# Down products in threes and twos, and a larger carry-over in the column stage: a fused spectral filter and gated MLP

## The chip, the cores and the metric

The kernel runs on one core of a Trainium2 chip. The metric is the device time of one execution in microseconds (us); times given as a median come from three runs. One further execution was taken by the profiler: its time is 1315.97 us, and the span that the trace covers is 1314.2 us. All stamps of the trace are microseconds from the start of that span.

## What is computed

The reference mixes two branches, cut here to what matters (S = 2048 tokens, D = 576, hidden width 4608, all float32):

```python
X = rfft2(A_x, axes=(-2, -1))                 # 2048 x 576
a = irfft2(X * (w_r + 1j * w_i), (S, D))      # spectral branch
h = gelu(B_x @ w_gate) * (B_x @ w_up)         # 2048 x 4608
b = h @ w_down
g = sigmoid((A_x * gate_w).sum(-1, keepdims=True))
y = g * a + (1 - g) * b
```

## The kernel before, in words

**Matmul branch.** TensorE does the products of B in float32 by splitting operands into a high and a low part. Hidden columns come in pairs of 128-wide blocks, tokens in two halves of 1024. The first two pairs of the first half are done plainly (`normal`). The other 34 (16 pairs of the first half, 18 of the second) are the *groups* of `products(b, k)` (L1397): the gate and up products of a pair with two times 512 tokens are made from **seven products** in the manner of Strassen, named in the loop at L1440 `a11, a12, s2, s3, s1, a22, s4`. The text calls them the first to the seventh. Each has two halves (s = 0, 1), each half is 7 matmuls of 128x512 into one PSUM bank (`seven`, six at L1390 and one at L1392). Partial results are copied from PSUM by ScalarE (`copy`, whose records carry L237): after the first product both halves are copied from one pair of banks into the other (`px<-pgu` or `pgu<-px`), after the third and the fourth into `xraw`. The second product goes on adding to the banks that the first one's copies read, and the fourth to the banks that the third one's copies read, so the second product's half s waits for the first product's copy of half s, and the fourth's for the third's.

**Down products.** A finished group gives eight *downs* (`down`, L992), 12 matmuls of 128x288 each (L975) into one of two PSUM buffers `pdn`. ScalarE evicts a down with the factor 1 - g (`stg<-pdn`, L1008) into one of four `stg` buffers, and GpSimd's queue issues the transfer that adds it to the sum `yd` in DRAM (`put`, L990). The eight downs of a group are carried in the list `pend` and done in the next group, so many after each product as `downs` (L1439) says. The opening group and the last one have rows of their own.

**Weights.** `prep` makes the weight tile of a product three products ahead: VectorE forms sums (L1362), ScalarE the high part (`gub<-low` or `slot<-low`, L237), VectorE the low part (L1377), and SP's queue fetches tails (L1369).

**Spectral branch.** It is written as Python generators that hand out a few VectorE and ScalarE instructions at a time: rows of the transform, then a *column stage* (`columns`, L291) whose 128-point transforms are 32 small TensorE products (L352, also into `pdn`), then the inverse rows for tokens 0 to 1023 (h = 0) and 1024 to 2047 (h = 1). At the end of each, `adds` (L700) scales eight blocks by g and adds them to `yd` through GpSimd's queue (L715); with h = 0 every second block is scaled by ScalarE (L712) and the others by VectorE (L714), out of five places that are used in turn.

**What sets the order.** Nothing reorders at run time: each engine runs its instructions in the order in which this program writes them. Between pieces of TensorE work (half a product, or a down) stands a *gap* (`gap`, `dealt`, L785). There the credit, which grows by 1.08 times the TensorE time passed and falls by what VectorE work costs, is cut to `cap` (2.0 us), and while it is positive the spectral generators give out instructions; `yield None` ends a generator's turn in that gap. In the column stage (`ops["ahead"]`) a second generator (`beside`) is served first, and a down's eviction is put off to the end of its gap. In that stage `HOLD` = 3 empty turns stand before the fourth step's next operand.

**The end.** In the last group the rest of the spectral work is handed out after the sixth product (`while gens`); then SP's queue loads blocks 12 to 15 of `yd` (`load_last(1)`, L1034), and the last eight downs (`finale`) are added to them on VectorE (L1045) and stored.

Of the kernel before, what the change touches and what calls it, by code (L numbers as in the profile page):

```python
# [28 lines left out]
UNIT = ROWS // 4  # L29
RATE = 1.08  # L30
STEP = 8
HOLD = 3
FIRST = 2
APART = (13, 14, 16, 17)
PAIRS = ((2, 3, 4, 5), (6, 7, 8, 9), (10, 11, 12, 13), (14, 15, 16, 17), (0, 1))
# [126 lines left out]
def _build(nc, tc, a):  # L162
    with ExitStack() as ctx:
# [127 lines left out]
        def columns():  # L291
# [90 lines left out]
            def beside():  # L382
                while not ops.get("turn"):
                    yield None
                yield from forward(1)
                for d in range(2):
                    yield from backward(d)
                    yield from forward(d + 2)
                for d in range(2, 4):
                    yield from backward(d)  # L390
# [11 lines left out]
            end = gub[BLOCK[1]][:, 2304:2560]  # L402
# [15 lines left out]
            yield from step()  # L418
            side.append(beside())
            ops["ahead"] = True  # L420
            for kb in range(16):
                was, more = kb > 0, kb + 1 < 16
                v = product(0, kb, xh, xl)
                if was:
                    copy(yh, vs)
                yield from step()
                copy(zr, v[:, 1, :NK])
                copy(t0, v[:, 0, :NK])
                yield from step()
                if was:  # L430
                    vec.tensor_tensor(yl, vs, f(yh), ALU.subtract)
                vec.tensor_tensor(zi, t0, zr, ALU.subtract)
                vec.tensor_tensor(zr, t0, zr, ALU.add)
                yield from step(1.67 if was else 0.91)
                turned(vs, z, 1.0)
                u = product(1, kb - 1, yh, yl) if was else None
                yield from step()
                if was:
                    copy(two(tile_of(kb - 1)), u[:, :, :NK])
                    done[0] = kb - 1  # L440
                vec.tensor_tensor(z, z, w0, ALU.mult)
                vec.tensor_tensor(vs, vs, w1, ALU.mult)
                yield from step(1.52)
                if more:
                    if kb == 3:
                        yield from waits(HOLD)
                    while made[0] < (kb + 1) // 4:
                        yield None
                    copy(xh, tile_of(kb + 1))
                vec.tensor_tensor(z, z, vs, ALU.add)  # L450
                vec.tensor_tensor(vs2[:, 0], zr, zi, ALU.add)
                vec.tensor_tensor(vs2[:, 1], zr, zi, ALU.subtract)
                at(1, lambda kb=kb: load_ww(kb + 1, 0))
                at(2, lambda kb=kb: load_ww(kb + 1, 1))
                yield from step(1.67)
                if more:
                    vec.tensor_tensor(xl, tile_of(kb + 1), f(xh), ALU.subtract)
                yield from step(0.76)
                yield from waits(STEP - 7)
# [11 lines left out]
            done[0] = 15  # L471
            yield None
            ops["ahead"] = False
            for c in side.pop():
                yield c
            for e in range(2):
# [118 lines left out]
        def waits(n):  # L595
            for _ in range(n):
                yield None
# [167 lines left out]
        cap = [2.0]  # L765
# [296 lines left out]
        ops = {}  # L1062
# [336 lines left out]
        def products(b, k):  # L1399

            p, i = b.groups[k]
            j = p * NT + 2 * i
            u, u3 = ([xraw[:, 2 * q + s] for s in range(2)] for q in range(2))
            made = {}
            opening, end, turn = k == 0, k == len(b.groups) - 1, (p, i) == (0, NBLK - 1)
            if opening:
                at(6, lambda: credit.__setitem__(0, credit[0] - 2.0))
                for q in range(2 * len(PAIRS) - 2):
                    t = (free_low[:, 0:7 * P] if q % 2 == 0 else wtb[:, 0:7 * P]).rearrange("p (m k) -> p m k", m=7)
                    for n, fn in zip((-4, 6, 8, 9, 10), tail_piece(q + 2, t)):  # L1410
                        at(max(1, n + 12 * q), fn)

            def finish(name, x, o):
                g, v = x
                hold = made[name] = []

                def mult():
                    vec.tensor_tensor(o, o, v, ALU.mult)
                    credit[0] -= 0.69

                def gelu():
                    act.activation(o, g, AF.Gelu_apprx_tanh)

                wants = dict(c21=extra[1:], c22=extra[:1]).get(name, base)
                if end and name in ("c21", "c12"):
                    gelu()
                    seq((name, k), (1, mult), *split_h(o, hold, wants, True))
                else:
                    soon = 0 if end else 1
                    high, low = (fn for _, fn in split_h(o, hold, wants))  # L1430
                    late = name in ("c22", "c12") and not end
                    seq((name, k), (1 + late, gelu), (2 + (soon if name != "c21" else 0) + late, mult), (4 + soon + late - end, high), (5 + 2 * soon + late, low))

            def add(o, v):
                vec.tensor_tensor(o, o, v, ALU.add)
                credit[0] -= 0.69

            fore, acc = ([f() for f in fs] for fs in ((ps_gu, ps_gu), (lambda: ps_x(0), lambda: ps_x(1)))[::1 - 2 * (k % 2)])
            downs = (0, 0, 0, 0, 0, 1, 1) if opening else (2, 2, 2, 2, 2, 0, 0) if end else (1, 1, 1, 1, 1, 1, 2)  # L1439
            for n, (name, nd) in enumerate(zip(("a11", "a12", "s2", "s3", "s1", "a22", "s4"), downs)):  # L1440
                m = n + 3
                b.prep(k + m // 7, m % 7)
                if n == 0 and k:
                    b.load_d(k)
                if n == 4:
                    w, x = dns[:, j % 4:j % 4 + 2], b.both
                    copy(w[:, :, 0], x)

                    def rest_of(w=w, x=x):
                        vec.tensor_tensor(w[:, :, 1], x, f(w[:, :, 0]), ALU.subtract)  # L1450
                        credit[0] -= 1.35

                    seq(("dn", j), (5, rest_of))
                if n == 3 and opening:
                    b.more()
                if n == 0:
                    b.load(k + 1, "r11", "r21")
                elif n == 3:
                    b.load(k + 1, "r22")
                elif n == 4:  # L1460
                    b.load(k + 1, "r12")
                if n == 4:
                    fore = [ps_x(s) for s in range(2)] if k % 2 else [ps_gu() for _ in range(2)]
                ps = acc if n in (2, 3, 5) else fore
                for s in range(2):
                    soon = opening and n in (0, 2)
                    b.seven(ps[s], k, n, name, s, n in (0, 4), (lambda n=n, s=s: copy((acc, None, u)[n][s], ps[s])) if soon else None)
                    if n in (0, 2, 3) and not soon:
                        copy((acc, None, u, u3)[n][s], ps[s])
                    elif n in (4, 6):  # L1470
                        at(0 if end else 1, lambda x=(u3, u)[n // 2 - 2][s], y=ps[s]: add(x, y))
                if turn:
                    ops["turn"] = True
                    if n == 6:
                        for q, e in enumerate(ye):
                            at(60 + 6 * q, lambda e=e: pl.dma_start(yd[e[1]], ye[e], accum_op=ALU.add, max_dma_last_dim=D))
                    assert ops["kept"]
                    at(2, lambda name=name: swap(name))
                if n in (1, 4, 5, 6):
                    finish(*{1: ("c11", fore, gl[0]), 4: ("c22", u3, u3[0]), 5: ("c21", acc, gl[1]), 6: ("c12", u, u[0])}[n])  # L1480
                for _ in range(nd):
                    if pend:
                        down(*pend.pop(0))
                if end and n == 5:
                    while gens:
                        credit[0] = 1.0
                        gap()
                    load_last(1)
            due(("dn", j))
            for tb, names in ((1, ("c21", "c22")), (0, ("c11", "c12"))):  # L1490
                d = (p, i, tb, tuple((j + q, made[names[q]], (names[q], k)) for q in range(2)))
                pend.extend((d, t) for t in range(4))
# [207 lines left out]
```

## Time and profile before

| | before |
|---|---|
| median of 3 runs (lowest to highest) | 1316.6 us (1315.26 to 1317.08) |
| the profiled execution: time, span | 1315.97 us, 1314.2 us |
| granted TensorE clock over the span | 0.997 |
| TensorE busy | 1300.6 us, 99% of the span, 7210 matmuls |
| VectorE, ScalarE, GpSimd busy | 1136.1, 832.7, 308.1 us |
| HBM read, written | 157.87, 137.88 MB |

A row of the timeline reads: start, duration, engine, line, operation, what is written from what, shapes, how many instructions are merged in it, and in brackets how long the engine had been idle before and what ended that. PE is TensorE, DVE VectorE, ACT ScalarE, POOL GpSimd, SP SyncE. Matmuls overlap, so the time between two starts, not the duration, says what one costs.

### The profile page before, as it was taken

What the parts mean: (1) busy time and instruction counts of PE and PEld (TensorE: products, weight loads), DVE (VectorE), ACT (ScalarE), POOL (GpSimd) and SP (SyncE); (2) the same over time, 40 slices, a digit from 0 to 9 for tenths busy, and PEclk for the clock granted to TensorE, in tenths of its full rate; (3) what the DMA queues carried; (4) which work ended last, traced back from release to release, by engine and by line L of the source; (5) the groups of instructions that cost most, each with busy time, mean ns of one, the idle gap of its engine ahead of it and who ended that gap; (6) DMA issues with size and microseconds to landing.
All of it is one profiled execution on the core that took longest, in us unless ns stands there. A gap on an engine that the chain in (4) does not pass through costs nothing.

```text
span 1314.2 us, 20538 instructions
## 1 busy us (share of the span) xinstructions
PE 1300.6 (99%) x7210; PEld 1152.4 (88%) x7210; DVE 1136.1 (86%) x1734; ACT 832.7 (63%) x1405; POOL 308.1 (23%) x392
## 2 busy tenths in 40 slices
PE   9999999999999999999999999999999999999996
PEld 7888888888888888888888888888888888888895
DVE  7899999988999988778878968767999997999974
ACT  5565665657565667768677876867656557556551
POOL 0011121212121111124310333333333314121131
PEclk9999999999999999999999999999999999999998
DMA  9779999896777799969985999999999979877789
GB/s 351 239 210 235 259 262 241 180 291 132 140 143 148 141 328 364 298 181 279 364 264 176 211 271 213 217 223 223 199 171 174 177 163 216 191 142 142 141 172 232
DMA packets 202392, 285.94 MB, mean 218 GB/s; under 512 B 18160, under 2 KB 118640, under 8 KB 201392
## 3 DMA queue, kind: packets, MB, share of 16 engines
q0 software_dynamic: 64848, 110.13, 48.7%
q1 hardware_dynamic: 137008, 174.06, 41.1%
q8 instruction: 56, 0.92, 0.3%
q10 hardware_dynamic: 432, 0.44, 0.1%
q14 instruction: 48, 0.39, 0.1%
HBM read 157.87 MB, written 137.88 MB: 225 GB/s over the span
## 4 chain that ended last, share of the span: by engine, by line
PE 91%; issue 4%; DMA 2%; POOL 1%; ACT 1%; DVE 0%; DVEq 0%; POOLq 0%; ACTq 0%; SPq 0%
PE pdn L975 32%; PE px L1390 23%; PE pgu L1390 23%; PE px L1392 4%; PE pgu L1392 4%; PE pdn L352 2%; POOL yd L990 1%; DMA yd<-wtb 1%; PE px L911 1%; DMA yd<-low 1%; PE pgu L911 0%; DMA low<-yd 0%; PE pgu L891 0%; PE pgu L892 0%; PE px L891 0%
## 5 line engine op out<-in xcount | busy, mean ns | idle before, releaser
L1008 ACT ACTIVATE stg<-pdn,omg 128x576 f32<-128x576 f32 x276 | 204.8, 743 | 327.5 <-PE pdn L975 206.5
L990 POOL DMA_DIRECT2D yd<-stg x232 | 201.6, 870 | 817.4 <-ACT stg L1008 787.3
L975 PE MATMUL pdn<-dn,hb 128*128 128x288 f32 x1356 | 199.5, 294 | 0.3 <-ACT rows L237 0.2
L975 PEld LDWEIGHTS pdn<-dn,hb 128*128 128x128 f32 x1356 | 191.7, 188 | 8.6 <-ACT rows L237 0.5
L1390 PE MATMUL pgu<-xhi,gub 128*128 128x512 f32 x480 | 149.2, 392 | 0.0
L975 PEld LDWEIGHTS pdn<-dn,ext 128*128 128x128 f32 x816 | 122.9, 189 | 17.1 <-DVE low L1045 7.4
L975 PE MATMUL pdn<-dn,ext 128*128 128x288 f32 x816 | 130.2, 295 | 7.0 <-DVE low L1045 7.0
L1390 PE MATMUL pgu<-til,gub 128*128 128x512 f32 x516 | 131.9, 391 | 0.0
L975 PE MATMUL pdn<-dn,gub 128*128 128x288 f32 x816 | 130.0, 295 | 0.0
L237 ACT ACTIVATE gub<-low 128x512 fp32r<-128x512 f32 (+1 forms) x163 | 101.0, 621 | 28.7 <-DVE low L1362 23.1
L975 PEld LDWEIGHTS pdn<-dn,gub 128*128 128x128 f32 x816 | 116.1, 189 | 0.0
L1377 DVE TENSOR_TENSOR gub<-low,gub 128x512 fp32r<-128x512 f32 x151 | 103.5, 685 | 8.5 <-ACT gub L237 6.9
L1390 PEld LDWEIGHTS pgu<-til,gub 128*128 128x128 f32 x516 | 94.5, 188 | 17.8
L1390 PE MATMUL px<-xhi,gub 128*128 128x512 f32 x344 | 106.9, 392 | 0.6 <-ACT xraw L237 0.6
L1390 PE MATMUL px<-til,gub 128*128 128x512 f32 x396 | 101.3, 391 | 0.0
L1390 PEld LDWEIGHTS pgu<-xhi,gub 128*128 128x128 f32 x480 | 86.4, 188 | 14.7 <-ACT px L237 0.3
L1390 PE MATMUL pgu<-xlo,gub 128*128 128x512 f32 x240 | 93.6, 390 | 0.0
L1390 PEld LDWEIGHTS px<-til,gub 128*128 128x128 f32 x396 | 72.3, 188 | 13.5
L1390 PEld LDWEIGHTS px<-xhi,gub 128*128 128x128 f32 x344 | 62.0, 188 | 11.9 <-ACT xraw L237 1.0
L975 PE MATMUL pdn<-dn,hx 128*128 128x288 f32 x444 | 70.2, 294 | 0.0
L1362 DVE TENSOR_TENSOR low<-low 128x512 f32<-128x512 f32 x98 | 67.4, 687 | 1.1 <-DMA low<-ws 0.3
L1390 PE MATMUL px<-xlo,gub 128*128 128x512 f32 x172 | 67.1, 390 | 0.0
(309 smaller groups left out, 2765.5 us busy)
## 6 DMA issues: line engine op xcount, KB each, us to landing
yd<-stg POOLq DMA_DIRECT2D x232, 288.0 KB, 5.3
low<-ws SPq DMA_DIRECT2D x114, 256.0 KB, 5.4
gub<-tails SPq DMA_DIRECT2D x179, 128.0 KB, 5.1
gub<-wd SPq DMA_DIRECT2D x68, 288.0 KB, 5.6
tails<-wtb SPq DMA_DIRECT2D x28, 448.0 KB, 5.6
ye<-stg POOLq DMA_DIRECT2D x32, 288.0 KB, 5.8
yd<-ye POOLq DMA_DIRECT2D x32, 288.0 KB, 8.0
slot<-tails SPq DMA_DIRECT2D x59, 128.0 KB, 4.9
```

The source lines that it names most:

```text
L237: act.activation(o, i, AF.Copy)
L352: pe.matmul(v[:, al, :NK], cc[d][2 * al + q], two(x)[:, al], start=n == 0, stop=n == 2)
L911: pe.matmul(ps[j][s], w[:, l, k, cs[s]], x0k, start=k == 0 and l == 0 and x is xhi, stop=k == 3 and x is xlo)
L975: pe.matmul(ps[half], h[:, l, c], d[:, q, half * HD:(half + 1) * HD], start=part == 0 and n == 0, stop=part == 1 and n == 2)
L990: pl.dma_start(yd[u], o, accum_op=ALU.add)
L1008: out = lambda: put(u, lambda o: act.activation(o.rearrange("p (c k) -> p c k", c=2), v[:, :, 0:HD], AF.Copy, scale=omg[:, u:u + 1]), i == ...
L1362: vec.tensor_tensor(o, p, q, ALU.subtract)
L1377: vec.tensor_tensor(v[:, 0:5:4], x, f(v[:, 1:4:2]), ALU.subtract)
L1390: pe.matmul(ps, l, x[:, t], start=first and t == 0 and q == 0, stop=False, skip_group_check=True)
L1392: pe.matmul(ps, w[:, 512 + P * s:512 + P * (s + 1)], xt, start=False, stop=True, skip_group_check=True)
```

## The change

Three edits. In groups that are neither the opening nor the last one, `downs` is replaced: outside the column stage three downs follow the second product, three the fifth and two the seventh; in the column stage it stays at one after each and two after the seventh. `popped` counts what was done, so that a group in which the stage begins or ends still does eight. The credit's cap is 3.0 in the column stage and 2.0 again after it. `HOLD` and its three empty turns are gone. Since lines went and came, L-numbers of the changed program differ by -1 to +3.

```diff
-HOLD = 3
...
             ops["ahead"] = True
+            cap[0] = 3.0
             for kb in range(16):
...
-                    if kb == 3:
-                        yield from waits(HOLD)
                     while made[0] < (kb + 1) // 4:
...
             ops["ahead"] = False
+            cap[0] = 2.0
...
+            popped = 0
             for n, (name, nd) in enumerate(zip(("a11", "a12", "s2", "s3", "s1", "a22", "s4"), downs)):
...
+                if not (opening or end):
+                    nd = (n + 1 + n // 6 if ops.get("ahead") else (0, 3, 3, 3, 6, 6, 8)[n]) - popped
+                    popped += max(0, nd)
                 for _ in range(nd):
                     if pend:
                         down(*pend.pop(0))
```

**First place: GpSimd's queue at the end of the program.** Before, the last twelve transfers into `yd`; L715 are the spectral branch's adds, L990 the downs' (`yd_151` to `yd_158` are the blocks 8 to 15):

```order
L990 DMA yd_151<-stg_84 128x576
L715 DMA yd_153<-wtb 128x576
L990 DMA yd_152<-stg_85 128x576
L715 DMA yd_154<-wtb 128x576
L715 DMA yd_155<-wtb 128x576
L990 DMA yd_153<-stg_86 128x576
L990 DMA yd_154<-stg_87 128x576
L715 DMA yd_156<-low 128x576
L715 DMA yd_157<-low 128x576
L715 DMA yd_158<-tmp 128x576
L715 DMA yd_151<-tmp 128x576
L715 DMA yd_152<-tmp 128x576
```

The last twelve of the changed program (L714 are the adds, L989 the downs'):

```order
L714 DMA yd_158<-tmp 128x576
L714 DMA yd_151<-tmp 128x576
L989 DMA yd_153<-stg_86 128x576
L989 DMA yd_154<-stg_87 128x576
L989 DMA yd_155<-stg_84 128x576
L989 DMA yd_156<-stg_85 128x576
L989 DMA yd_157<-stg_86 128x576
L989 DMA yd_158<-stg_87 128x576
L989 DMA yd_151<-stg_84 128x576
L989 DMA yd_152<-stg_85 128x576
L989 DMA yd_153<-stg_86 128x576
L989 DMA yd_154<-stg_87 128x576
```

Before, the adds are the very last; now ten downs, more than a group's worth, follow the last add.

**Second place: TensorE in the group that the adds of h = 0 fall into.** Before, from the down behind the second product to the fourth product (`px0`, `px1` are the banks of halves 0 and 1):

```order
L975 MATMUL pdn_10202<-dn_75,hb0_78 128x288 x6
L975 MATMUL pdn_10202<-dn_75,hb1_80 128x288 x6
L1390 MATMUL px0_10135<-til1_335,gub2_73 128x512 x6
L1392 MATMUL px0_10135<-til1_335,gub2_73 128x512
L1390 MATMUL px1_10136<-til1_335,gub2_73 128x512 x6
L1392 MATMUL px1_10136<-til1_335,gub2_73 128x512
L975 MATMUL pdn_10246<-dn_75,ext_911 128x288 x6
L975 MATMUL pdn_10246<-dn_75,gub2_73 128x288 x6
L1390 MATMUL px0_10135<-til1_335,slot_74 128x512 x6
L1392 MATMUL px0_10135<-til0_334,slot_74 128x512
L1390 MATMUL px1_10136<-til1_335,slot_74 128x512 x6
L1392 MATMUL px1_10136<-til0_334,slot_74 128x512
```

The changed program, in the group that its adds fall into, from the second of the three downs behind the second product to the fourth product (`pgu_9855` and `pgu_9856` are here the two banks):

```order
L974 MATMUL pdn_9926<-dn_75,hb2_79 128x288 x6
L974 MATMUL pdn_9926<-dn_75,hx_159 128x288 x6
L974 MATMUL pdn_9945<-dn_75,ext_911 128x288 x6
L974 MATMUL pdn_9945<-dn_75,gub2_73 128x288 x6
L1389 MATMUL pgu_9855<-til1_335,slot_74 128x512 x6
L1391 MATMUL pgu_9855<-til1_335,slot_74 128x512
L1389 MATMUL pgu_9856<-til1_335,slot_74 128x512 x6
L1391 MATMUL pgu_9856<-til1_335,slot_74 128x512
L1389 MATMUL pgu_9855<-til1_335,gub1_72 128x512 x6
L1391 MATMUL pgu_9855<-til0_334,gub1_72 128x512
L1389 MATMUL pgu_9856<-til1_335,gub1_72 128x512 x6
L1391 MATMUL pgu_9856<-til0_334,gub1_72 128x512
```

The down that stood between the third and the fourth product is gone from there; both write the same two banks.

**Third place: ScalarE in the same two groups.** Before (L712 scale blocks for the adds, L1008 evict downs, `xraw<-px` are the copies of the third and then of the fourth product):

```order
L712 ACTIVATE wtb<-rows,gs 128x576
L237 ACTIVATE xraw<-px_10135 128x512
L237 ACTIVATE gub_72<-low 128x2x256
L712 ACTIVATE low<-rows,gs 128x576
L237 ACTIVATE xraw<-px_10136 128x512
L1008 ACTIVATE stg_84<-pdn,omg 128x576
L712 ACTIVATE wtb<-rows,gs 128x576
L237 ACTIVATE hb_78<-gl_81 128x512
L237 ACTIVATE xraw<-px_10135 128x512
L237 ACTIVATE gub_73<-low 128x2x256
L712 ACTIVATE wtb<-rows,gs 128x576
L237 ACTIVATE xraw<-px_10136 128x512
```

The changed program (L711, L1007 and L236 are the same lines; L1421 is the GELU):

```order
L1007 ACTIVATE stg_86<-pdn,omg 128x576
L1421 ACTIVATE gl_81<-px_9853 128x512
L711 ACTIVATE low<-rows,gs 128x576
L1007 ACTIVATE stg_87<-pdn,omg 128x576
L711 ACTIVATE wtb<-rows,gs 128x576
L1007 ACTIVATE stg_84<-pdn,omg 128x576
L711 ACTIVATE wtb<-rows,gs 128x576
L236 ACTIVATE xraw<-pgu 128x512
L236 ACTIVATE hb_79<-gl_81 128x512
L236 ACTIVATE gub_73<-low 128x2x256
L236 ACTIVATE xraw<-pgu 128x512 x2
L236 ACTIVATE slot<-low 128x2x256
```

Before, the fourth and last L712 stood ahead of the fourth product's second copy; now it stands ahead of the third product's first copy.

## The prediction

> **What bounds the kernel now.** I read the page first, then the chain of waits, then the timeline wherever TensorE stood still. On the page:
>
> ```profile
> PE 1300.6 (99%) x7210; PEld 1152.4 (88%) x7210; DVE 1136.1 (86%) x1734; ACT 832.7 (63%) x1405; POOL 308.1 (23%) x392
> ```
>
> TensorE sets the time nearly everywhere, so an edit is worth what it changes in TensorE's standing still, or in the cost of a matmul. No matmul is added or removed. The place where TensorE stands still longest is shown by the end of the chain of waits:
>
> ```profile
> 1285.89 7.29 DMA yd<-low
> 1293.24 5.95 DMA low<-yd
> ```
>
> The last adds of the spectral branch are in flight to 1293.2; only then can SP load those sums for the last downs. In TensorE's timeline (start first, in brackets the idle time):
>
> ```profile
> 1288.01 0.95 PE L975 MATMUL pdn<-dn,ext 128*128 128x288 f32 x6
> 1288.80 0.95 PE L975 MATMUL pdn<-dn,gub 128*128 128x288 f32 x6
> ...
> 1290.39 0.95 PE L975 MATMUL pdn<-dn,gub 128*128 128x288 f32 x6
> 1291.68 1.06 PE L975 MATMUL pdn<-dn,ext 128*128 128x288 f32 x6 [0.34 <-DVE low L1045]
> 1292.58 0.95 PE L975 MATMUL pdn<-dn,gub 128*128 128x288 f32 x6
> 1300.17 1.81 PE L975 MATMUL pdn<-dn,ext 128*128 128x288 f32 x6 [6.64 <-DVE low L1045]
> 1301.78 1.64 PE L975 MATMUL pdn<-dn,gub 128*128 128x288 f32 x6
> 1303.22 1.07 PE L975 MATMUL px<-dn,hb 128*128 128x288 f32 x6
> ```
>
> Six matmuls take 0.79 from start to start (1288.01 to 1288.80). The five steps from 1290.39 to 1303.22 take 12.83 instead of 5 x 0.79 = 3.95, so this stall costs **8.9 us**. After the idle 6.64, two sixes took 1.61 and 1.44: 1.47 of the 8.9 is slow matmuls behind a long pause.
>
> **The change part by part, against the profiled 1315.97.**
>
> *The spectral branch ends earlier.* `HOLD`'s three empty turns and the lower cap go; in GpSimd's queue ten downs follow the last add, more than a group. So the load of blocks 12 to 15 no longer waits for an add. What is late next there is the last down's transfer to block 15, which was issued here:
>
> ```profile
> 1270.18 0.86 POOL L990 DMA_DIRECT2D yd<-stg  x1 [0.42 <-ACT stg L1008]
> ...
> yd<-stg POOLq DMA_DIRECT2D x232, 288.0 KB, 5.3
> ```
>
> It lands at about 1275.5, and with 5.95 for the load that is 1281.4, 8 us ahead of the first down of the finale that needs it (ends 1289.6). That covers it: **-8.9**.
>
> *The column stage itself* must pack the same work into less TensorE time:
>
> ```profile
> 560.00:875.00 315.00, 314.75 (x1786) 280.88 (x1785) 251.35 (x400) 238.78 (x401) 95.84 (x138) 1.00 0.94 242
> ```
>
> VectorE is busy 251 of 315 there (80%). Roughly 35 us, one group, goes; with that group's own VectorE work gone too it becomes about 84%, still under full, and TensorE idled only 0.25 in this stretch. I take 0, bounded by -0.25 and the price in the fourth rival.
>
> *Fewer changes between shapes.* A group, by the chain of waits:
>
> ```profile
> 1103.51 1.38 PE pgu L1390 x6
> ...
> 1105.12 1.36 PE pgu L1390 x6
> 1106.71 3.16 PE pdn L975 x24
> ...
> 1141.72 3.16 PE pdn L975 x24
> ```
>
> The half product behind a down takes 1.61 to the next half, the second half 1.59 (1105.12 to 1106.71). A change from downs to products so costs 0.02; seven a group become three. Of 32 groups that are neither first nor last, eight lie in the column stage (280 us of 35.0 each, 1106.71 to 1141.72): 24 x 4 x 0.022 = **-2.1** (0 if the 0.02 belongs to something else).
>
> *Copies that lose their cover.* This is the part that I hold against the change. Before, 1.58 of down lay between the first and the second product and between the third and the fourth, so a copy of half s had two pieces, 3.17, to finish in; now it has one half product, 1.59. Undisturbed it needs about 0.85 (0.25 from the end of TensorE's piece to ScalarE's start, as at 1273.67 to 1273.92 below, and 0.6 for itself) and costs nothing. But ScalarE runs in order, and the weight piece just ahead of it waits for VectorE:
>
> ```profile
> ACT gub L237 <- DVE low L1362: 23.1, 21, 2.8
> ...
> 314.06 0.95 PE L975 MATMUL pdn<-dn,hb 128*128 128x288 f32 x6
> 315.63 0.63 PE L1390 MATMUL px<-xhi,gub 128*128 128x512 f32 x2
> 315.71 0.63 ACT L237 ACTIVATE gub<-low 128x512 fp32r<-128x512 f32 x1 [2.40 <-DVE low L1362]
> 316.25 0.58 ACT L237 ACTIVATE pgu<-px 128x512 f32<-128x512 f32 x1
> ...
> 936.98 1.74 PE L975 MATMUL pdn<-dn,hb 128*128 128x288 f32 x12
> ...
> 938.24 0.58 ACT L237 ACTIVATE px<-pgu 128x512 f32<-128x512 f32 x1
> ```
>
> At 314 the second half of the first product ended at 314.06; the copy ended at 316.83. Under the new order the second product's second half is due at 314.06 + 1.59 = 315.65: a stall of 1.18 that the down hid. In the same way for all pairs outside the column stage I find eight places, at 314, 324, 359, 454, 489, 524, 902 and 937, with 1.18, 0.69, 0.41, 0.86, 1.56, 1.38, 1.69 and 0.25: **+8.0**. The VectorE work ahead of them is the same in both orders, moved by a gap or two, so I keep the sum; bounds are 0 (the lag falls elsewhere) and 11.
>
> *Third down of three.* It needs the first one's buffer:
>
> ```profile
> 1272.09 3.32 PE L975 MATMUL pdn<-dn,hb 128*128 128x288 f32 x24
> 1273.92 0.74 ACT L1008 ACTIVATE stg<-pdn,omg 128x576 f32<-128x576 f32 x1 [1.03 <-PE pdn L975]
> ```
>
> The first of these two ended at 1273.67, its eviction at 1274.66, and a third would start at 1275.25: 0.59 to spare. ScalarE must be late by more; bounded by 0 and 6 (a quarter of 48 places by 0.5), I take **+0.5**, near the quiet row.
>
> *The adds of h = 0* fall into another part of a group. Before:
>
> ```profile
> yd<-wtb POOLq DMA_DIRECT2D x9, 288.0 KB, 7.5
> ...
> 1084.27 0.59 ACT L1422 ACTIVATE gl<-pgu 128x512 f32<-128x512 f32 x1
> ...
> 1087.05 1.47 ACT L712 ACTIVATE low<-rows,gs 128x576 f32<-128x576 f32 x1
> 1088.90 0.74 ACT L1008 ACTIVATE stg<-pdn,omg 128x576 f32<-128x576 f32 x1
> 1090.00 0.85 POOL L990 DMA_DIRECT2D yd<-stg  x1 [2.63 <-ACT stg L1008]
> 1090.54 1.19 POOL L715 DMA_DIRECT2D yd<-wtb  x1
> 1098.03 1.47 ACT L712 ACTIVATE wtb<-rows,gs 128x576 f32<-128x576 f32 x1 [3.07 <-DMA yd<-wtb]
> 1099.08 0.39 PE L1392 MATMUL px<-til,gub 128*128 128x512 f32 x1
> 1099.36 0.63 ACT L237 ACTIVATE xraw<-px 128x512 f32<-128x512 f32 x1
> 1100.04 0.73 PE L1390 MATMUL px<-xhi,gub 128*128 128x512 f32 x2 [0.57 <-ACT xraw L237]
> ```
>
> The fourth L712 reuses the third add's place and waits until that transfer, issued at 1090.54, has landed. The copy behind it belonged to the fourth product and was needed by the sixth: TensorE lost 0.73 (0.96 from 1099.08 to 1100.04, where a matmul takes 0.23). Now the copy behind it is the third product's, which the fourth waits for. Counted from the end of the first of the three downs: 0.25 to its eviction, 0.74 for it, 0.59 GELU, 1.47 for the second L712, 0.74 for the next eviction, 0.36 and 0.54 in GpSimd's queue (as 1089.64 to 1090.00 and to 1090.54), 7.47 in flight, 1.47 for the fourth L712, 0.6 copy: 14.2. The fourth product is due after two downs and two halves, 3.16 + 3.18 = 6.3. That is 7.9, and 1.5 of slow matmuls as behind the 6.64 pause: **+9.4**, and **-0.7** for the old stall. VectorE waits there for another place too, but stands free before the copy is done. Behind the stalled fourth product all of TensorE's queue waits; the other engines catch up.
>
> Sum: 1315.97 - 8.9 - 2.1 + 8.0 + 0.5 + 9.4 - 0.7 = 1322.2. The median of the runs lies 0.6 above the profiled execution, so **1322.8**.
>
> **The rivals.** (1) *ScalarE's queue is short at the joints.* In threes, evictions no longer stand between a product and its copies. If that lets VectorE and ScalarE come to the joints with less than 1.59 of lag, the 8.0 is gone, and one eviction, 0.7, goes from the chain at the adds: 1322.8 - 8.7 = 1314.1, against 1316.6 faster by 0.2%. It decides from the point where the lag at those eight places falls under 1.59. Against it: at 314 ScalarE waited 2.40 for VectorE and not for an eviction. (2) *The adds' transfers land sooner.* The nearest quick row for this size is a plain store:
>
> ```profile
> yd<-stg SPq DMA_DIRECT2D x16, 288.0 KB, 2.2
> ```
>
> With 2.2 for 7.47 the stall is 2.6 without slow matmuls: 1322.8 - 9.4 + 2.6 = 1316.0. Against it stands the median of 7.5 of these very transfers. The Trainium skill, "DMA: Bandwidth & Descriptors", section "Anatomy of one DMA — SWDGE (gpsimd) path", fits 2.0 us plus bytes over 436e3 to a transfer issued by GpSimd, by my estimate 2.7 us for 288 KB; the sum by it would be 1316.5. The trace here has 7.5, nearly three times that. (3) *Both together*: 1307.3. (4) *The stage becomes VectorE's.* Were each of its 32 small products 0.2 late, 6.4 more: 1329.2. Against it the 84%. That the branch would not end earlier is excluded by the order of GpSimd's queue.
>
> The Trainium skill also says in "TensorE: Matmul & The Clock Gate", section "The HAM clock gate (the "warmup" mystery)", that the array's clock is halved after an idle window of about 3.4 us and returns after as long a busy one. The 1.47 behind the 6.64 is of that kind; by the page the pause at the adds would cost 1.7 behind it, 1323.0 in all, and several pauses of one or two us nothing.
>
> **How the numbers follow.** Forecast 0.57, rival 1 0.20, rival 2 0.10, rival 3 0.05, rival 4 0.08. About 0.2%, 2.6 us, can be told from no change: faster is under 1314.0, slower over 1319.2. Rival 1 at 1314.1 is half faster, half same; rival 3 is faster, and a fifth of rival 2: 0.10 + 0.05 + 0.02 = 0.17. Same: 0.10 + 0.08 and 0.05 of the forecast, if the copies cost 4 instead of 8: 0.23. Slower 0.60. The forecast's own range is 1318 to 1327 (copies 4 to 11, flight 5.3 to 8.0 as the rows for transfers into `yd` have it). To hold 8 in 10, the range takes in rivals 1 and 2 to 1312 and part of rival 4 to 1328:
>
> ```profile
> yd<-ye POOLq DMA_DIRECT2D x32, 288.0 KB, 8.0
> ```
>
> **What would show it.** Right: the finale's downs 0.79 a six without the 6.64; the half behind a down still 1.61; waits of the second and fourth product for ScalarE's copies, in sum near 8, and one of about 8 us behind the fourth scaling of h = 0. Wrong: no single TensorE wait over 3 us near 1050, TensorE's waits for copies under 3 in all, or a long wait still ahead of the finale.

## The result, and the profile after

The changed kernel takes **1333.2 us** (median of four runs, 1332.26 to 1334.14); the kernel before takes 1316.35 beside it (four runs, 1315.26 to 1317.08). The ratio is 1.0128, 95% interval 1.0115 to 1.0141: slower by about 17 us. The prediction had the sign and the two largest terms, the end and the adds; its 1322.8 was short by 10 us, and the result lies outside its range, which ended at 1328. The profiled execution of the changed kernel took 1332.48 us with a span of 1330.7, at a granted clock of 0.996.

The page's first line, busy time and instructions of each engine:

```profile
PE 1305.1 (98%) x7210; PEld 1153.0 (87%) x7210; DVE 1137.7 (85%) x1734; ACT 831.4 (62%) x1405; POOL 308.4 (23%) x392
```

All engines run as many instructions as before, and VectorE, ScalarE and GpSimd are busy as long as before, within 2 us. TensorE is busy 4.5 us longer, in matmuls that run slowly behind pauses; the rest of the 17 us are the pauses between its matmuls. What TensorE waited for (engine, line, what released it, then us in all, times, longest), of before the largest, and of after:

```profile
PE pdn L975 <- DVE low L1045: 7.0, 2, 6.6
```

```profile
PE pgu L1389 <- ACT xraw L236: 8.9, 2, 7.9
PE px L1389 <- ACT pgu L236: 5.2, 6, 1.6
PE pgu L1389 <- ACT px L236: 2.1, 2, 1.6
...
PE pdn L351 <- DVE tmp L431: 1.3, 1, 1.3
PE pdn L974 <- ACT stg L1007: 1.2, 2, 0.8
```

One wait of the end is gone, and waits for ScalarE's copies (L236) stand all over the program. To put each microsecond in its place I took from both traces, for every matmul, the time from its start to the next one's start, less what it is in undisturbed work (0.227 us for 512 columns, 0.132 for 288, 0.1345 for the stage's 290), and summed the excess by place (the program's first 10 us, 2.6 in both, are left out):

| place | before | after | difference | predicted |
|---|---|---|---|---|
| groups before the column stage | 0.1 | 3.9 | +3.8 | +6.1 (six of the eight copies) |
| column stage | 0.8 | 5.1 | +4.4 | 0 |
| behind the stage, up to the adds of h = 0 | 0.3 | 7.7 | +7.4 | +1.9 (two of the eight copies) |
| adds of h = 0 | 0.8 | 10.3 | +9.5 | +8.7 |
| last two groups and finale | 9.0 | 0.6 | -8.4 | -8.9 |
| single steps of 0.04 or less, all places | 4.1 | 4.3 | +0.2 | -2.1 |

The differences sum to 16.9 and the two profiled executions lie 16.5 apart, so the table holds all of it to 0.4. The prediction's column sums to 5.7; with its +0.5 for the third downs that is its 6.2.

**The end.** The finale in TensorE's timeline (start, duration, engine, line):

```profile
1313.79 0.95 PE L974 MATMUL pdn<-dn,ext 128*128 128x288 f32 x6
...
1319.36 0.95 PE L974 MATMUL pdn<-dn,gub 128*128 128x288 f32 x6
1320.15 0.97 PE L974 MATMUL px<-dn,hb 128*128 128x288 f32 x6
```

Eight steps in 6.36, 0.795 each: the 6.64 that stood here is gone, as foretold.

**The adds of h = 0**, timelines of ScalarE, GpSimd and TensorE together:

```profile
1062.73 0.74 ACT L1007 ACTIVATE stg<-pdn,omg 128x576 f32<-128x576 f32 x1 [1.80 <-issue]
1063.85 1.42 ACT L711 ACTIVATE low<-rows,gs 128x576 f32<-128x576 f32 x1
1065.18 0.73 ACT L1007 ACTIVATE stg<-pdn,omg 128x576 f32<-128x576 f32 x1
...
1067.78 0.85 POOL L989 DMA_DIRECT2D yd<-stg  x1 [1.98 <-issue]
1068.32 1.18 POOL L714 DMA_DIRECT2D yd<-wtb  x1
1068.65 0.39 PE L1391 MATMUL pgu<-til,slot 128*128 128x512 f32 x1
1075.02 1.34 ACT L711 ACTIVATE wtb<-rows,gs 128x576 f32<-128x576 f32 x1 [4.11 <-DMA yd<-wtb]
1076.27 0.58 ACT L236 ACTIVATE xraw<-pgu 128x512 f32<-128x512 f32 x1
1076.90 2.93 PE L1389 MATMUL pgu<-til,gub 128*128 128x512 f32 x6 [7.87 <-ACT xraw L236]
...
1080.06 2.26 PE L1389 MATMUL pgu<-til,gub 128*128 128x512 f32 x6
```

These are the links of the prediction in its order; their lengths differ, as the account of the prediction below says. The add issued at 1068.32 has landed by 1075.02, the fourth scaling reuses its place, the copy of the third product stands behind it, and the fourth product waits 7.87. Seven matmuls then take 3.16 (1076.90 to 1080.06) instead of 1.59.

**Copies that lost their cover.** The place at 314 of the kernel before, now:

```profile
315.39 0.68 DVE L1361 TENSOR_TENSOR low<-low 128x512 f32<-128x512 f32 x1
...
315.93 0.39 PE L1391 MATMUL px<-til,gub 128*128 128x512 f32 x1
316.11 0.63 ACT L236 ACTIVATE gub<-low 128x512 fp32r<-128x512 f32 x1 [2.28 <-DVE low L1361]
316.64 0.58 ACT L236 ACTIVATE pgu<-px 128x512 f32<-128x512 f32 x1
317.28 0.74 PE L1389 MATMUL px<-xhi,gub 128*128 128x512 f32 x2 [0.95 <-ACT pgu L236]
```

From 315.93 to 317.28 are 1.35 where 0.23 is usual: 1.12 lost, and 1.18 was foretold. Behind the stage there is more of it than foretold:

```profile
913.44 0.39 PE L1391 MATMUL px<-til,gub 128*128 128x512 f32 x1
913.66 0.64 ACT L236 ACTIVATE ext<-gl 128x512 fp32r<-128x512 f32 x1
914.20 0.70 ACT L236 ACTIVATE rows<-wtb 128x289 f32<-128x289 f32 x1
914.70 0.69 ACT L236 ACTIVATE pgu<-px 128x512 f32<-128x512 f32 x1
915.44 0.73 PE L1389 MATMUL px<-xhi,gub 128*128 128x512 f32 x2 [1.61 <-ACT pgu L236]
```

Here it is the inverse rows' own copy (`rows<-wtb`) and an operand's that stand ahead of the product's copy.

**The column stage.** VectorE's timeline, TensorE's at the same time, and the busy time in the stage (in this order PE, PEld, DVE, ACT, POOL):

```profile
618.20 1.56 DVE L266 TENSOR_TENSOR rows<-low,rows 128x580 f32<-128x580 f32 x2 [0.93 <-ACT low L251]
619.67 1.55 DVE L266 TENSOR_TENSOR rows<-rows,low 128x580 f32<-128x580 f32 x2
621.14 0.68 DVE L959 TENSOR_TENSOR hb<-gl,hb 128x512 fp32r<-128x512 f32 x1
621.75 0.76 DVE L431 TENSOR_TENSOR tmp<-wtb,tmp 128x580 fp32r<-128x580 f32 x1
622.56 0.40 PE L351 MATMUL pdn<-tmp 128*128 128x290 f32 x1 [1.26 <-DVE tmp L431]
```

```profile
565.00:846.00 281.00, 277.49 (x1578) 247.18 (x1577) 232.00 (x372) 216.70 (x367) 83.59 (x125) 1.00 0.92 248
```

VectorE is busy 232 of 281 there, 83%, which the prediction had as 84% and took for harmless. The small product starts at 620.86, and the operand that its third matmul needs (L431) stands in VectorE's queue behind four sums of the second generator (L266) and a product's own work. VectorE itself had stood idle for 0.93 ahead of these sums, for a step of ScalarE (L251), and the first half of that step (L250) had waited 0.90 for VectorE's sums before it (L259): the two hand work to each other.

**Longer runs of one shape.** Three downs in a quiet group:

```profile
1141.29 0.95 PE L974 MATMUL pdn<-dn,hb 128*128 128x288 f32 x6
...
1144.45 0.98 PE L974 MATMUL pdn<-dn,ext 128*128 128x288 f32 x6
...
1146.06 1.54 PE L1389 MATMUL pgu<-til,gub 128*128 128x512 f32 x6
```

The first two downs take 3.16 (1141.29 to 1144.45), the third 1.61 instead of 1.58.

### The profile page after: what moved, and what is told of

Its sections match the earlier page's. It is cut to its first block, busy times and chain, and to the rows that moved or that the text cites. A ratio compares the mean times of both kernels' runs of the same rounds, so it can differ in the third digit from the quotient of the medians.

```text
span 1330.7 us, 20521 instructions
## 1 busy us (share of the span) xinstructions
PE 1305.1 (98%) x7210; PEld 1153.0 (87%) x7210; DVE 1137.7 (85%) x1734; ACT 831.4 (62%) x1405; POOL 308.4 (23%) x392
## 4 chain that ended last, share of the span: by engine, by line
PE 71%; issue 13%; DVE 4%; DMA 4%; POOL 4%; ACT 4%; SPq 0%; POOLq 0%; DVEq 0%; ACTq 0%
PE pdn L974 25%; PE pgu L1389 17%; PE px L1389 17%; PE pgu L1391 3%; POOL yd L989 3%; PE px L1391 3%; DMA yd<-stg 2%; PE pdn L351 1%; POOL yd L714 1%; DMA gub<-wd 1%; ACT stg L1007 1%; DMA rows<-away 1%; DVE rows L266 1%; DMA home<-rows 1%; PE px L910 1%
## 5 line engine op out<-in xcount | busy, mean ns | idle before, releaser
L1007 ACT ACTIVATE stg<-pdn,omg 128x576 f32<-128x576 f32 x276 | 204.7, 742 | 311.8 <-PE pdn L974 228.3
L989 POOL DMA_DIRECT2D yd<-stg x232 | 202.4, 879 | 799.2 <-ACT stg L1007 764.8
L1389 PE MATMUL pgu<-til,gub 128*128 128x512 f32 x516 | 133.8, 395 | 8.9 <-ACT xraw L236 8.9
L236 ACT ACTIVATE gub<-low 128x512 fp32r<-128x512 f32 (+1 forms) x163 | 100.9, 621 | 41.4 <-DVE low L1361 34.7
L974 PEld LDWEIGHTS pdn<-dn,ext 128*128 128x128 f32 x816 | 119.3, 188 | 4.1
L1391 PE MATMUL pgu<-til,gub 128*128 128x512 f32 x172 | 67.3, 391 | 0.0
```

What stands on the lines that cost most here:

```text
L236: act.activation(o, i, AF.Copy)
L974: pe.matmul(ps[half], h[:, l, c], d[:, q, half * HD:(half + 1) * HD], start=part == 0 and n == 0, stop=part == 1 and n == 2)
L989: pl.dma_start(yd[u], o, accum_op=ALU.add)
L1007: out = lambda: put(u, lambda o: act.activation(o.rearrange("p (c k) -> p c k", c=2), v[:, :, 0:HD], AF.Copy, scale=omg[:, u:u + 1]), i == ...
L1389: pe.matmul(ps, l, x[:, t], start=first and t == 0 and q == 0, stop=False, skip_group_check=True)
L1391: pe.matmul(ps, w[:, 512 + P * s:512 + P * (s + 1)], xt, start=False, stop=True, skip_group_check=True)
```

## The experiments

The theory after the result has four parts. (A) Copies of the first and third product wait because no down stands behind those products. (B) The adds of h = 0 stall because the scaling that waits for its place stands ahead of a copy. (C) The two edits of the column stage cost TensorE time in the stage because VectorE is late there. (D) The same two edits remove the stall at the end. Rivals: that threes of downs choke ScalarE by their evictions; that the waits in the stage are ScalarE's or a transfer's; that the waits behind the stage come from its earlier end alone. Times below are medians, the ratio is to runs of the kernel before on the same chip (medians 1316.6, 1317.1, 1317.1 and 1316.6 in the four groups of runs).

| run | us | ratio, 95% interval |
|---|---|---|
| threes and twos alone | 1328.59 | 1.0087, 1.0072 to 1.0102 |
| stage's edits alone | 1318.30 | 1.0014, 1.0005 to 1.0023 |
| twos behind the first, third, fifth and seventh product | 1319.07 | 1.0017, 1.0008 to 1.0027 |
| changed kernel, scalings spaced | 1322.67 | 1.0040, 1.0025 to 1.0055 |
| stage's edits, scalings spaced | 1311.86 | 0.9964, 0.9951 to 0.9976 |
| no HOLD, scalings spaced | 1315.19 | 0.9984, 0.9975 to 0.9992 |
| cap 3.0, scalings spaced | 1314.58 | 0.9979, 0.9967 to 0.9991 |
| scalings spaced alone | 1315.21 | 0.9984, 0.9975 to 0.9993 |
| stage's edits with cap 2.25, spaced | 1314.02 | 0.9976, 0.9966 to 0.9986 |
| stage's edits with cap 2.5, spaced | 1313.45 | 0.9976, 0.9965 to 0.9988 |
| stage's edits, half of the four-point sums, spaced | 1307.42 | 0.9929, 0.9915 to 0.9942 |
| changed kernel, threes only before the stage, spaced | 1315.80 | 0.9996, 0.9986 to 1.0006 |

**1. The two halves of the change.** Threes and twos alone: the changed kernel with `HOLD` and without the higher cap.

```diff
-            cap[0] = 3.0
...
+                    if kb == 3:
+                        yield from waits(3)
...
-            cap[0] = 2.0
```

> The new places of the downs alone; the column stage keeps its cap of 2.0 and its three empty turns. Theory (a copy that has lost the down behind the first and the third product has half the time, and TensorE waits for it; the column stage and the adds have prices of their own): the stall ahead of the finale stays near 8.9, the column stage costs nothing more, copies outside the stage cost 8 to 11 us, and the second scaling of h = 0 that waits for a transfer stands ahead of a third-product copy here, 2 to 4: about 1327 us, 10 or more slower than before. Rival (the larger carry-over puts VectorE behind, and its lag makes the waits for copies, before and after the stage alike): 1316 to 1319, with at most the four waits seen ahead of the stage (3.8 us).

1328.59. What TensorE waits for:

```profile
PE px L1389 <- ACT xraw L236: 7.4, 2, 7.1
PE pdn L974 <- DVE low L1044: 4.8, 2, 2.7
PE px L1389 <- ACT pgu L236: 3.7, 5, 1.0
```

The long wait at the adds, the copies and the stall at the end all stand beside each other. By place: 3.9 before the stage, 0.8 in it, 2.1 behind it, 10.3 at the adds, 7.1 at the end. Behind the stage it is 2.1, near the 1.9 that the prediction read out of the trace before; in the changed kernel it is 7.7. That the total lies near the 1327 I expected is in part luck: the copies cost 6.0 where I had 8 to 11, the adds 10.3 where I had 2 to 4, and the end 7.1 where I had 8.9.

The stage's edits alone: downs one after each product, everywhere.

```diff
-                    nd = (n + 1 + n // 6 if ops.get("ahead") else (0, 3, 3, 3, 6, 6, 8)[n]) - popped
+                    nd = n + 1 + n // 6 - popped
```

> Cap 3.0 and no empty turns, with the downs where they were, one after each product and two after the seventh. Theory: the stall ahead of the finale goes (-8.4), the column stage's own waits come (+4.4), no waits for first- and third-product copies since a down covers each again, adds about as before: about 1312.4, faster than before by 4. Rival (the stage edits put VectorE behind for the rest of the program): the waits for copies behind the stage stay, 7 us, and it ends at 1319 or later.

1318.30, between the two forecasts. Timelines of ScalarE and TensorE at the adds:

```profile
1060.08 1.32 ACT L711 ACTIVATE wtb<-rows,gs 128x576 f32<-128x576 f32 x1 [4.26 <-DMA yd<-wtb]
...
1061.94 2.93 PE L1389 MATMUL pgu<-til,gub 128*128 128x512 f32 x6 [3.94 <-ACT xraw L236]
```

Part D holds: the end costs 0.8 (9.0 before). Part C holds: the stage costs 4.5 (0.8 before). What I had wrong is that the adds would be as before: they cost 6.5, since the earlier stage puts them into another part of a group even without threes. With the stage's edits in place, then, only some 4 of the changed kernel's 10.3 need the threes; the threes alone give 10.3 as well, so either half of the change is enough to move the adds to a bad place. The copies behind the stage, which the rival had at 7, cost 1.4.

**2. Is it the missing cover, or the bunching?** Downs in twos behind the first, third, fifth and seventh product: bunched too, but downs follow each product whose copies the next one waits for.

```diff
-(0, 3, 3, 3, 6, 6, 8)[n]
+(2, 2, 4, 4, 6, 6, 8)[n]
```

> All of the change, but outside the column stage the eight downs follow the first, third, fifth and seventh product in twos, so that two downs stand between a copied product and the one that adds to the same banks. Theory (the lost cover is the price, not the bunching): waits for copies near 0, the wait of about 8 at the adds near 0 since its copy is the fourth product's again, the end stall gone, the stage at +4.4: about 1312 us. Rival (downs in bunches and fewer changes between shapes are what costs): 1325 or more, since there are four changes a group here as against three, and seven before.

1319.07. Before the stage TensorE loses 0.1 (3.9 in the changed kernel), behind it 1.1 (7.7). Part A holds, and the rival that bunching as such chokes ScalarE falls, for twos: the stage (7.8) and the adds (5.9) are what is left. The total was a miss, 7 over the 1312 I expected, and so were the adds, which I had near 0: two downs stand there between the copied product and the next, 3.17 us, and TensorE still stood still for 4.2.

**3. The adds.** The changed kernel, and the last four scalings of h = 0 stand four gaps apart instead of one, so that each place has been written out before it is used again.

```diff
-                    n = count[0] + (1 + len(todo_t) % 2 if h else 1)
+                    n = count[0] + (1 + len(todo_t) % 2 if h else 4 if t > 3 else 1)
```

> The changed kernel with the last four blocks of the adds of h = 0 handed out four gaps apart instead of one, so that their places' transfers have landed. Theory (TensorE's 8.0 us wait and the 2.2 us of slow matmuls behind it come from ScalarE waiting there for the third add's transfer): both go, 1333.2 - 10.2 = 1323.0; the spectral branch ends some 20 us later and still ahead of the finale. Rival (the wait is VectorE's lag, and the transfer only lies beside it): no less than 1330.

1322.67; the adds cost 0.65 instead of 10.3, and every other place is as it was (4.0, 4.5, 7.8, 0.6). Part B holds with its price.

**4. Which of the stage's two edits does what.** In this and the next group the scalings are spaced, so that the adds add nothing (0.0 in all of them). First both edits, downs as before:

> The column stage's two edits alone (cap 3.0, no HOLD), downs one after each product as before, and the last four scalings of h = 0 four gaps apart. Theory: the end stall is gone (-8.4), the stage costs TensorE some 4.4, the scalings no longer hold up the fourth product (before lost 0.8 there, so -0.7), and nothing is lost for copies: 1316.6 - 8.4 + 4.4 - 0.7 = 1311.9, TensorE's waits from 1024 to 1100 under 1 us in all. Rival: the scalings stall wherever they fall in this order, spaced or not, as they did with the stage's edits alone (4.1 + 2.4): 1318.

1311.86, as foretold, and **the lowest median of all versions that compute the whole**: 0.9964 of the kernel before. (With cap 3.0 alone and with the lower caps of 5. the intervals overlap with this one.) Each edit alone, and neither; the differences are to the kernel before, beside the spacing:

```diff
-                    if kb == 3:
-                        yield from waits(HOLD)
```

> Only HOLD is taken out (cap 2.0, downs as before), and the last four scalings of h = 0 stand four gaps apart. In the order of work the stage then ends where it ended before; its fourth and fifth small products come some 3 us earlier only. Theory: the three empty turns gave VectorE and ScalarE the time that they lack there; without them the small products behind the fourth step wait 1.43 and 1.0, as in the changed kernel: 1316.6 - 0.7 + 2.4 = 1318.3, with the end stall of about 8.9 still there. Rival: the higher cap alone makes the small products wait: 1315.9.

```diff
+            cap[0] = 3.0
...
+            cap[0] = 2.0
```

> Only the cap is raised to 3.0 in the column stage (HOLD kept, downs as before), and the last four scalings of h = 0 stand four gaps apart. In the order of work the stage ends at the same place as with both edits. Theory: the cap alone brings the earlier end (-8.4), and of the stage's 4.4 the 2.4 behind the fourth step stay away: 1316.6 - 8.4 - 0.7 + 2.0 = 1309.5. Rival: the stage's waits come from the cap: 1311.9 or more.

> The kernel before, and only the last four scalings of h = 0 stand four gaps apart. Theory: the 0.7 that TensorE lost behind the fourth scaling goes and the end stays as it was, with the long wait ahead of the last downs: 1315.9. Rival: the later scalings push the adds of h = 1 and so the load at the end: 1318 or more.

Without `HOLD` 1315.19, with the spacing alone 1315.21: at the cap of 2.0, taking the three empty turns out does nothing, neither in the stage (0.8 and 0.8) nor at the end (7.0 and 7.8). My theory, that they give VectorE the time that it lacks and that the run without them costs 1318.3, falls at this cap. With the cap alone the end is free (0.0) and the stage costs 5.7, so the cap by itself brings both the gain and a loss. What TensorE waits for there (L-numbers as in the kernel before):

```profile
PE pdn L352 <- DVE tmp L458: 1.9, 2, 1.0
...
PE pdn L352 <- DVE tmp L432: 1.3, 1, 1.3
```

The wait of 1.3 is the one shown above for L431, but it tells nothing about `HOLD`: its small product stands ahead of the three turns in the program. Around the next two, which the turns precede, 1.15 was lost with both edits and 0.3 is lost here, so under the high cap the turns do give time at that place; but 0.9, 1.2 and 1.2 are lost later (at 672, 737 and 778), and the 1309.5 that I expected was missed by 5. Its runs reach from 1311.61 to 1316.66 and those with both edits from 1311.24 to 1314.08; whether `HOLD` matters for the total under the high cap, these do not tell. The spacing alone leaves the stall at the end and gains 0.16%.

**5. What the stage waits for.** A lower cap, 2.25 and 2.5 in place of 3.0:

> The stage's two edits with a cap of 2.25 instead of 3.0, downs one after each product, and the last four scalings of h = 0 four gaps apart. In the order of work the stage ends 30 us earlier than before (35 with 3.0), and the last add stands where it stands with 3.0. Theory: the waits in the stage come from more than two us of VectorE work handed out in one gap; with 2.25 they fall from 5 us over before to 2 or less and the end stall stays away: 1309.5. Rival: they come from the shorter stage itself and stay: 1312 or more.

> As the run with a cap of 2.25, with a cap of 2.5; the stage ends 32 us earlier than before, and the third step's second small product stands where it stands with 2.25. Theory: between the two, nearer to 2.25, as the 1.43 behind the third step stays away: 1310. Rival: as with 3.0, 1312.

1314.02 and 1313.45, for 1309.5 and 1310 expected: the times are the rival's, and handing out less at once does not bring the loss down. That the shorter stage is the reason, as the rival has it, fits, but was not shown apart. The end stays free, the wait behind the third step is gone, and others have come, so that the stage costs 8.4 and 7.0. Timelines of VectorE, ScalarE and TensorE with 2.25:

```profile
748.29 0.46 DVE L433 TENSOR_TENSOR wtb<-rows,wtb 128x290 f32<-128x290 f32 x1
748.85 0.69 ACT L250 ACTIVATE wtb<-wtb 64x580 f32<-64x580 f32 x1 [2.76 <-DVE wtb L433]
...
750.25 0.74 ACT L1007 ACTIVATE stg<-pdn,omg 128x576 f32<-128x576 f32 x1
751.04 1.50 PE L974 MATMUL pdn<-dn,hb 128*128 128x288 f32 x6 [2.30 <-ACT stg L1007]
```

VectorE is late again (L433), ScalarE waits 2.76 for it with a down's eviction behind, which in the stage is put off to the end of its gap, and the next down waits for that. The caps can't be ranked by these runs: from 2.25 to 3.0 the intervals overlap, and with one and the same order in the stage single executions show it at 4.5 (the stage's edits alone, and 3.), 4.9 (6., below), 7.8 (2.) and 7.7 (both edits, spaced; in it 3.8 are a pause of 2.0 and the slow matmuls behind it, where a copy stands behind a step of ScalarE that waits 2.88 for a reload). For that part the rival of a transfer holds: the reload came late in two of these executions and in time in the others. To test VectorE itself: both edits with cap 3.0, and the 64 sums and differences of the second generator's four-point steps on half of their columns; the other half is left out. The order stays the same.

```diff
-                vec.tensor_tensor(o, p, q, op)
+                vec.tensor_tensor(o[:, 0:NK], p[:, 0:NK], q[:, 0:NK], op)
```

> The stage's two edits with cap 3.0, downs one after each product, the last four scalings of h = 0 four gaps apart, and the 64 sums and differences of the column stage's four-point steps on 290 of their 580 columns: the other columns are left out, so some 20 us of VectorE work are gone from the stage while the order stays the same, instruction for instruction. Theory: VectorE is late at the small products; the waits 1.43, 1.04 and 0.54 in front of and behind them go, and the one of 2.05, where ScalarE waits for a reload, stays: 3 us less than with all columns, 1309. Rival: the small products wait for ScalarE and for transfers: 1311.9 as with all columns.

1307.42 (1306.69 to 1309.08), 4.4 less than with all columns. VectorE's row of the stage (the third engine column) and TensorE's waits in the whole program:

```profile
560.00:840.00 280.00, 279.63 (x1590) 249.67 (x1590) 221.09 (x376) 219.06 (x371) 84.74 (x127) 1.00 0.93 250
```

```profile
PE pgu L1544 <- DVE gate L1540: 1.5, 1, 1.5
PE px L1389 <- ACT pgu L236: 0.5, 1, 0.5
PE pgu L1389 <- ACT px L236: 0.5, 1, 0.5
PE pdn L351 <- DMA gub<-col: 0.3, 1, 0.3
```

The stage costs 1.1. VectorE's share falls only from 82% (with all columns, 560 to 845) to 79%, and nearly all waits of the stage go, the one for ScalarE's eviction too (0.9). Part C holds, and further than I had it: that wait, under ScalarE's name, was VectorE's lateness handed on. The wait behind the reload, which I expected to stay, is gone as well; as it comes and goes between executions of one order, its absence here shows nothing, and the fair comparison for the stage is 4.5 to 1.1.

**6. Behind the stage.** The run of 3., and threes only in the groups before the stage.

```diff
-n + 1 + n // 6 if ops.get("ahead") else
+n + 1 + n // 6 if "ahead" in ops else
```

> The changed kernel with the last four scalings of h = 0 four gaps apart, and threes only in the groups before the column stage: in it and behind it one down follows each product and two the seventh. Theory: the waits for copies behind the stage, 2.7 at its end and 5.0 later in the changed kernel, come from the missing down and fall to about 1.2 as in the run with the stage's edits alone; those before the stage, 3.9, stay: 1322.7 - 6.5 = 1316.2. Rival: they come from the stage that ends a group earlier and meets other work there, and stay: 1322.7. A saving by longer runs of one shape would show in the groups before the stage and doesn't: TensorE's small excess stays at 5.2 in all.

1315.80. Behind the stage TensorE loses 1.3 (7.8 with threes there), before it 4.9, of which 0.8 is one wait for a transfer. So the 7.7 behind the stage needs both halves of the change: without the threes it is 1.3 to 1.4, without the earlier end 2.1.

## Why the prediction was right or wrong

- **The end, -8.9: right.** -8.4 came. Nothing else was late there but one wait of 0.36 for an eviction.
- **The adds, +9.4 - 0.7: right in the chain, and its length in part by luck.** From the end of the first of the three downs (0.25 ahead of its eviction, so 1062.5) to the fourth product's start at 1076.9 it took 14.4 where 14.2 was worked out; the stall is 8.03 (7.9 foretold). But two links were off and made up for each other: from the end of the second eviction (1065.91) to the add's issue (1068.32) GpSimd's queue took 2.41 for 0.90, and the transfer landed after 6.70 for 7.47; the rest of the chain was 0.5 shorter. The slow matmuls behind the stall cost 2.3 (1.5): their price was taken from downs behind another pause.
- **The column stage, 0: wrong, and the first of the two big misses.** That it "becomes about 84%, still under full" was the reason. The share was right (83%) and the conclusion was not: a share over 281 us says nothing of the moment at which one operand is due. The fourth rival had the mechanism and a bound of 6.4; 4.4 came, with single waits of 1.4, 1.0, 1.2 and 0.5 and not 32 small ones. It was set against the forecast, with 0.08, though nothing in the forecast excluded it: it should have been added.
- **Copies, +8.0: mechanism right, size wrong, the second big miss.** "The VectorE work ahead of them is the same in both orders, moved by a gap or two" failed twice. Before the stage 3.8 came for 6.1: the places at 314 (1.12 for 1.18), 454 and 524 are there, those at 324, 359 and 489 (0.69, 0.41 and 1.56) are not, and one at 291 is new. Behind the stage, which ends a group earlier, other work meets the joints: 7.4 for 1.9. With the threes alone the sum there would have been right (2.1), most of it at one of the two places foretold (1.8 for the 1.69 at 902).
- **Fewer changes of shape, -2.1: wrong.** Nothing was gained. In the twelve groups between the opening and the stage, the first seven matmuls of each run of products cost 1.9 over the quiet value before and 0.9 after, as worked out; but the third down of each three costs 0.7, and 0.4 more is spread over the longer runs. The step "A change from downs to products so costs 0.02" took a run's start as all that depends on its length.
- **Third down, +0.5: not there as a wait.** TensorE waits for an eviction twice, once in the stage and once in the last group, never within a three.
- **Rivals.** The first (joints short of lag) and the second (transfers land sooner) fall: the copies' waits are there, and the adds' transfers took a median of 8.0 for 7.5 before:

```profile
yd<-wtb POOLq DMA_DIRECT2D x9, 288.0 KB, 8.0
```

The Trainium skill's fit in "DMA: Bandwidth & Descriptors", section "Anatomy of one DMA — SWDGE (gpsimd) path", gives 2.7 us for this size by the estimate in the prediction; the trace differs, 8.0, and decides.

- **The range.** Its upper end came from bounding one term at a time. The two misses, +4.4 in the stage and +5.5 behind it, both push up and both need the stage's earlier end; a range that lets two terms go wrong for one reason would have come near the result: +9.9 on 1322.2 is 1332.1, where the profiled execution has 1332.48. That they alone come so near is luck, since the other errors (copies before the stage -2.3, changes of shape +2.3, adds +0.8, end +0.5, third down -0.5) nearly cancel.

## What to carry to other kernels

A wait that disappears from a queue tells only half; work that ends earlier also lands elsewhere, and every place that it passes or enters (here the stage itself, the groups behind it, the adds) has to be priced again in its new neighbourhood, not with the numbers of the old one. A piece of work between a producer and the next user of its buffer is cover, and grouping such pieces for longer runs gives the cover away. An engine at 83% over a stretch can be the one that sets it, if operands fall due in bursts.

## What the runs showed of the hardware

- *Slow matmuls behind a pause.* The windows view shows the granted clock behind four pauses (the number behind the engines' columns): of 8.03 us in the changed kernel, of 2.04 with both stage edits and spaced scalings, of 2.46 with cap 2.5, and of 2.46 at the same place with cap 2.25.

```profile
1076.90:1081.90 5.00, 5.00 (x12) 3.97 (x13) 4.02 (x8) 2.59 (x5) 0.67 (x1) 0.53 1.10 195
```

```profile
761.10:766.10 5.00, 4.97 (x20) 4.21 (x21) 1.17 (x3) 4.89 (x8) 2.50 (x4) 0.66 0.89 260
```

```profile
750.20:754.00 3.80, 3.59 (x21) 3.24 (x22) 3.77 (x8) 3.14 (x7) 2.55 (x4) 1.00 1.13 287
```

```profile
751.40:754.80 3.40, 3.40 (x15) 3.21 (x14) 3.37 (x7) 1.95 (x5) 1.96 (x3) 0.50 1.12 249
```

Behind 8.03 the clock was 0.53, and 11 matmuls of 512 columns took 0.35 to 0.60 from start to start, most of them 0.43, instead of 0.227: 2.3 in all. Behind 2.04 it was 0.66 and cost 1.8 in all; behind 2.46 it was 1.00 and cost 0.1 in the one run, and 0.50 and 1.7 in the other. So between two and two and a half us the length alone does not decide. The Trainium skill, "TensorE: Matmul & The Clock Gate", section "The HAM clock gate (the "warmup" mystery)", has the clock fall to half after one idle window of some 3.4 us, and the windows run freely. What came behind the first pause and the third agrees with that; the slow stretches behind 2.04 us and the second 2.46, pauses shorter than such a window, do not.

- *The third of three downs.* Its first two matmuls take 0.143 and one later 0.140 where the second down's take some 0.132, in all 24 threes of the groups before the stage alike. Why is not settled; it was not tried apart from the change.
